# Decoding float64 weights with three VectorE instructions a piece, w1 ahead of the late part of w2

## The chip, the cores and the metric

The kernel runs on one core of one Trainium2 chip. A core has a matrix engine (TensorE, in the profile PE for matmuls and PEld for weight loads), VectorE (DVE), ScalarE (ACT), GpSimd (POOL) and SyncE (SP), whose queue issues nearly all DMAs here. Each engine runs its own instructions strictly in their order, and semaphores make one engine wait for another. The metric is device time of one execution in microseconds; the median of three runs of the kernel before is 1156.33 us (1154.52 to 1156.69).

## What is computed

Linear attention with random features on 8 batches, 8 heads, 576 tokens, 64 channels and 128 features; then a token mixing of rank 32 with a residual; then a two-layer MLP with relu and a residual. Inputs of the attention are float32; U, V, w_ch1 (w1, 512 x 2048) and w_ch2 (w2, 2048 x 512) come as float64.

```python
def phi(x):
    proj = np.einsum('bhsd,md->bhsm', x, omega)
    sq = np.sum(x * x, axis=-1, keepdims=True) / 2.0
    h = proj - sq
    h = h - np.max(h, axis=-1, keepdims=True)
    return np.exp(h) / np.sqrt(m)
q_p, k_p = (phi(q_s), phi(k_s))
kv = np.einsum('bhsm,bhsd->bhmd', k_p, v)
z = np.sum(k_p, axis=2)
num = np.einsum('bhsm,bhmd->bhsd', q_p, kv)
den = np.einsum('bhsm,bhm->bhs', q_p, z)[..., None] + 1e-06
...
xt = x.transpose(0, 2, 1)
h = xt @ U @ V
u = x + h.transpose(0, 2, 1)
ch = np.maximum(u @ w_ch1, 0.0) @ w_ch2
return (u + ch).astype(np.float32)
```

## The kernel before

**Attention.** A unit is a pair of batches and two heads; there are 16. A round takes the keys of one unit and the queries of another through nine tiles of 128 rows, one tile of each a step, so 16 rounds make 144 steps (and seven more that finish). In a step TensorE projects both tiles (L500 to L502, once for each of the two parts), VectorE takes the maximum (L508, tile nm), ScalarE the exponentials (L515, tile e), TensorE multiplies keys with values (L412) or transposes the queries' features (L438), VectorE or ScalarE copies those (L443), and TensorE combines them with kv (L458). Every three steps VectorE turns raw keys or queries (L373), ScalarE rounds them (L377) and GpSimd subtracts for the remainder (L381). The table `DELAY` says how many steps after its own each operation stands in the program.

**Mixing.** When a pair of batches is done, `mixing` takes nine tiles through U and V between the steps, with its subtraction on GpSimd (L261; on VectorE for the last pair) and an addition on VectorE (L276), and stores u to DRAM.

**MLP.** u comes back in 12 chunks of 384 tokens. An *item* is one chunk and one of 16 blocks of 128 hidden channels: 12 matmuls of the first layer (L682 to L684, tile p_p, two buffers), relu with rounding on ScalarE (L687, tile gh), its remainder on VectorE (L688, tile gl) and 9 matmuls of the second layer (L700), which stand behind the next item's first layer. There are 192 items. The first four take blocks 0 and 1 of chunks 0 and 1, and then these two chunks share each block, so that a row block f of w2 is first used at item 2f.

**Decoding.** `decoding` is a generator over 35 *pieces* of up to 512 float64 a row: U, two of V, 16 of w1, 16 of w2. A piece is loaded by SP into raw (two buffers, words interleaved); ScalarE takes the absolute value of the high words as a float into mag (L111, two buffers); VectorE clamps (L127), shifts and masks (L128), puts the sign back (L131), takes the power of two of the result (L134) and multiplies the low word by it (L135, tile de); GpSimd adds de to mag (L149); ScalarE rounds the sum to the high part and GpSimd subtracts for the low part (L162 and L163, for the weights). The generator yields after every VectorE instruction, so an `advance` is one of them. `left` counts the advances allowed before the late part of w2, which takes the place in SBUF of the mixing's tiles: 6 empty ones and 60 instructions, 12 pieces (U, V, w1's 0 to 5, w2's 0 and 1, w1's 6). In attention two of three steps advance once, which uses them up by step 99. The other 23 pieces come in the MLP, five instructions an item, w1 and w2 in turn.

**Order.** A scheduler sets each engine's order from the program's dependences and its own estimate of times; VectorE's decoding instructions and some copies are pinned to the program's order.

Of the kernel before, what the change touches and what calls it, by code (L numbers as in the profile page):

```python
# [9 lines left out]
F32 = mybir.dt.float32  # L10
F32R = mybir.dt.float32r
U32 = mybir.dt.uint32
AF = mybir.ActivationFunctionType
# [10 lines left out]
#: High words of the least and the greatest float64 with a normal float32's exponent.  # L24
# [4 lines left out]
def performer_mlp_kernel(ctx: ExitStack, tc, q, k, v, omega, U, V, w1, w2, out):  # L29
    """phi(q) (phi(k)^T v) / den, then x + V^T U^T x and a relu MLP with a residual.  # L30

    float32 products run natively or as float32r passes over operands split exactly into a
    rounded high part and the remainder. U, V, w1 and w2 come as the bits of float64 and are
    rounded to float32. The 2 x 576 rows of a pair of batches make nine tiles of 128, the fifth
    with the last 64 rows of one batch and the first 64 of the next.
    """
# [17 lines left out]
    # Both feature maps carry 1 / sqrt(M), which the quotient drops when the guard grows by M.  # L54
# [42 lines left out]
    def decoding(jobs, late=0):  # L97
        """jobs: (load, n, finish...); load(raw) fills [P, n, 2] with the words of n float64 in each
        row, and each finish(w) runs in turn on the float32 [P, n]. Yields after every VectorE
        instruction; loads run ahead."""  # L100
        raws, mags = {}, {}

        def fetch(i):
            if i < len(jobs):
                raws[i] = dec.tile([P, PIECE, 2], U32, name="raw", bufs=RB)[:, : jobs[i][1], :]
                jobs[i][0](raws[i])

        def magnitude(i):
            if i < len(jobs):
                mags[i] = dec.tile([P, PIECE], F32, name="mag", bufs=2)[:, : jobs[i][1]]  # L110
                nc.scalar.activation(out=mags[i], in_=f32(raws[i][:, :, 1]), func=AF.Abs)  # L111

        for i in range(RB):
            fetch(i)
        for _ in range(late):
            yield
        magnitude(0)
        rest = []
        for i, job in enumerate(jobs):
            n = job[1]  # L120
            raw, m = raws.pop(i), mags.pop(i)
            low, high = raw[:, :, 0], raw[:, :, 1]
            e = dec.tile([P, PIECE], F32, name="de", bufs=2)[:, :n]
            # The float32 of the high word's bits in m; the rest is the low word in units of 2^-52
            # of its power of two.
            slots = [
                lambda: nc.vector.tensor_scalar(m, m, _LEAST, _MOST, ALU.max, ALU.min),  # L127
                lambda: nc.vector.tensor_scalar(  # L128
                    words(m), words(m), 3, 0x3FFFFFFF, ALU.logical_shift_left, ALU.bitwise_and
                ),  # L130
                lambda: nc.vector.scalar_tensor_tensor(  # L131
                    words(m), high, 0xC0000000, words(m), ALU.bitwise_and, ALU.bitwise_or
                ),
                lambda: nc.vector.tensor_scalar(words(e), words(m), 0xFF800000, None, ALU.bitwise_and),  # L134
                lambda: nc.vector.scalar_tensor_tensor(e, low, 2.0**-52, e, ALU.mult, ALU.mult),  # L135
            ]
            for j, slot in enumerate(slots):
                tc.keep_in_program_order(slot())
                if rest:
                    rest.pop(0)()  # L140
                if j == 3:
                    magnitude(i + 1)
                if j == 4:
                    fetch(i + RB)
                yield
            while rest:
                rest.pop(0)()
            rest = [
                lambda e=e, m=m: nc.gpsimd.tensor_tensor(out=m, in0=m, in1=e, op=ALU.add),  # L149
            ]  # L150
            rest += [lambda fn=fn, m=m: fn(m) for fn in job[2:]]
        while rest:
            rest.pop(0)()
            yield
# [16 lines left out]
    # What the first steps of the MLP need, then the pieces of w1 and w2 in turn.  # L171
    N1, FIRST = DF // PIECE * NC, 6
# [15 lines left out]
    # U in columns [high, high, low, high], a slot for each tile of each batch: four of the first  # L188
    # batch, the shared tile's two with zeros in the other batch's rows, four of the second.
# [22 lines left out]
    # V in rows [high, high, high, low]; the shared tile has a slot for each batch.  # L212
# [27 lines left out]
    # Instructions of the decoder before the first that needs the late part of w2.  # L240
    left = [6 + 5 * (1 + 2 + FIRST + AHEAD + 1)]
# [8 lines left out]
    def mixing(pair, x, last):  # L250
        """A tile of x may be written as late as the one before it is used. The last pair's has the
        more of VectorE and of the banks."""
# [68 lines left out]
    def fetch(c, raws):  # L321
        """A chunk of u in 32 x 32 blocks that VectorE turns: row 32 a + i holds, for each block of 32
        tokens, 32 channels of block a of its token i."""
        for cc, raw in enumerate(raws):
            for a in range(4):
                k = cc * P + a * BLK
                nc.sync.dma_start(
                    out=raw[a * BLK : (a + 1) * BLK, :].rearrange("i (b j) -> i b j", j=BLK),
                    in_=u_dram[c][:, k : k + BLK].rearrange("(b i) j -> i b j", i=BLK),
                )  # L330

# [6 lines left out]
    # The third unit comes before the first buffer is free; the second of x is, till then.  # L338
# [7 lines left out]
    def blocks(src, raw, unit, j):  # L346
        """A batch of two heads in 32 x 32 blocks that VectorE turns: row 64 h + 32 a + i holds, for
        each block of 32 tokens, 32 channels of half a of its token i."""
        pair, hp = unit
        for h in range(2):  # L350
            for a in range(2):
                r = h * D + a * BLK
                nc.sync.dma_start(
                    out=raw[r : r + BLK, j * S : (j + 1) * S].rearrange("i (b c) -> i b c", c=BLK),
                    in_=src[2 * pair + j, 2 * hp + h, :, a * BLK : (a + 1) * BLK].rearrange("(b i) c -> i b c", i=BLK),
                )

    class Part:
        """Keys or queries of a unit, in the first or the second place of a round."""
# [9 lines left out]
        def turn(self):  # L369
            """The next group of tiles with channels on the partitions."""  # L370
# [12 lines left out]
    class Keys(Part):  # L383
        """phi(k)^T [v, 1] of two heads and two batches."""
# [37 lines left out]
    class Queries(Part):  # L422
        """The attention's output for two heads and two batches, into x."""

        def __init__(self, i, place):
# [4 lines left out]
            # The two of the last round share a bank for each tile, others one for two tiles.  # L430
# [32 lines left out]
        def finish(self, s, x):  # L463
# [7 lines left out]
            if s == 4:  # L471
                # Heads, then batches, of which a row has its own.
# [14 lines left out]
    class Step:  # L487
        """A step of a round: a tile of two heads from each of its parts."""
# [15 lines left out]
        # exp(h - max(h)): |x|^2 / 2 is one number for a row, so h - max(h) is proj - max(proj).  # L504
# [14 lines left out]
        def group(self, i):  # L519
            """Part i, when a group of tiles begins."""  # L520
# [11 lines left out]
    # Each round has two of the 32 parts: a unit's queries come two rounds after its keys but for  # L532
    # the first, and the first and the last round have two of a kind.
# [8 lines left out]
    # The tensor engine's clock goes up before its first work comes.  # L542
# [7 lines left out]
    for vt, vm in values:  # L550
        # Values with a column of ones for the denominator; the shared tile has a row's values
        # in its batch's columns and zeros in the other's.
# [19 lines left out]
    NR = len(units)  # L572
    # How many steps after its own a step's operation comes in the program.
# [9 lines left out]
    for s in range(NR * NT + 7):  # L583
# [17 lines left out]
        elif t == 7:  # L601
            # The MLP's first tokens, where the last pair but one was.
# [6 lines left out]
        if s % 3:  # L609
            advance(decoder)  # L610
# [52 lines left out]
    class Chunk:  # L663
# [28 lines left out]
        def layer2(self, f, gh, gl):  # L692
# [4 lines left out]
            for t, po in enumerate(self.po):  # L697
                ts = slice(t * P, (t + 1) * P)
                for i, (g, w) in enumerate(((gh, h), (gh, l), (gl, h))):
                    step = nc.tensor.matmul(po, g[:, ts], w, start=(f + i == 0), stop=(f == NF - 1 and i == 2))  # L700
                    if (self.c, f) == (NCH - 1, NF - 1):
                        # The last rows leave a tile at a time.
# [16 lines left out]
    # Two chunks share the first pass over the weights while these are decoded, then one a pass.  # L719
# [10 lines left out]
    def end(i):  # L730
        """The second layer of step i, behind the first of step i + 1."""
# [33 lines left out]
    for i in range(begun, len(items)):  # L765
        c, f = items[i]
        advance(decoder, 5, True)
# [37 lines left out]
```

## Time and profile before

| | |
|---|---|
| median of three runs | 1156.33 us |
| the profiled execution, from first to last instruction (span) | 1154.0 us |
| TensorE matmuls busy | 1123.9 us |
| mean granted TensorE clock | 0.991 |
| attention, first projection of step 0 to that of step 143 | 8.4 to 316.3 us |
| first matmul of MLP item 0 | 327.5 us |
| last piece decoded by VectorE | 456 us |

The profile's lines are read in this way. A window's row gives, for a stretch in microseconds, its length and then each engine's busy time with its number of instructions, the granted TensorE clock, the busy share of the DMA engines and GB/s. A group's row gives line, engine, operation, output and inputs with shapes and count, then busy time, mean duration in ns, and the idle time of the engine just before such instructions with what ended it. A row of waits gives who waited for whom, the total, how often and the longest. Overlapping matmuls make a busy TensorE look fuller than it is, so the number of matmuls in a stretch is read with it.

### The profile page before, as it was taken

To read this page: it belongs to the slowest core of one execution; us is meant where nothing else is said; L and a number is where in the kernel's file an instruction comes from. 1 tells how busy PE (TensorE), PEld (TensorE's weight loads), DVE (VectorE), ACT (ScalarE), POOL (GpSimd) and SP (SyncE) were. 2 spreads that over 40 slices of the span, in tenths; PEclk is the share of its full clock that TensorE was granted. 3 is DMA by queue.
4 is the path that set the end of the run, shared out by engine and by line. 5 is a ranking of instruction groups with operands and counts; after the bars stand their busy time and mean duration, and the time that the engine had idled before them with its cause. 6 is when DMAs were issued, how large, how long until landed. Compare 5 with 4: busy or idle time off the path is not lost.

```text
span 1154.0 us, 17600 instructions
## 1 busy us (share of the span) xinstructions
PE 1123.9 (97%) x6481; PEld 1020.8 (88%) x6481; DVE 538.6 (47%) x1088; ACT 405.3 (35%) x1115; POOL 280.7 (24%) x261
## 2 busy tenths in 40 slices
PE   8989999999999889999999999999999999999998
PEld 7989889899978677999999999999999999999997
DVE  3889999998997998411212121221212121111211
ACT  4978889788842333211111111111111111111111
POOL 3446657645244555201001010100101010010000
PEclk7999999999999999999999999999999999999999
DMA  7787686774356332420303030030303001010100
GB/s 131 141 152 138 139 180 132 155 157 89 93 146 154 106 106 74 105 61 5 78 1 83 1 74 10 7 75 1 83 1 82 1 1 55 1 55 1 46 1 28
DMA packets 288661, 84.95 MB, mean 74 GB/s; under 512 B 270368, under 2 KB 270368, under 8 KB 288576
## 3 DMA queue, kind: packets, MB, share of 16 engines
q1 hardware_dynamic: 288512, 83.77, 31.8%
q8 instruction: 51, 0.84, 0.3%
q14 instruction: 34, 0.28, 0.1%
q0 software_dynamic: 64, 0.07, 0.0%
HBM read 64.91 MB, written 18.87 MB: 73 GB/s over the span
## 4 chain that ended last, share of the span: by engine, by line
PE 71%; DVE 10%; DMA 2%; issue 1%; SPq 1%; ACT 1%; POOL 0%; DVEq 0%; ACTq 0%
PE p_p L683 10%; PE p_n L700 10%; PE p_p L684 10%; PE p_p L682 10%; PE p_q L700 10%; PE p_m L700 5%; PE p_kv L700 5%; PE p_n L458 2%; DVE mag L131 2%; PE p_kv L412 2%; DVE de L134 2%; DVE mag L128 2%; PE p_p L500 1%; PE p_q L438 1%; PE p_p L502 1%
## 5 line engine op out<-in xcount | busy, mean ns | idle before, releaser
L688 DVE SCALAR_TENSOR_TENSOR gl<-p_p,gh 128x384 fp32r<-128x384 f32 x192 | 106.8, 556 | 522.2 <-ACT gh L687 521.9
L687 ACT ACTIVATE gh<-p_p 128x384 fp32r<-128x384 f32 x192 | 94.0, 490 | 570.1 <-PE p_p L684 569.1
L682 PE MATMUL p_p<-uh,w1h 128*128 128x384 f32 x768 | 258.5, 337 | 1.7 <-DVE gl L688 1.3
L683 PE MATMUL p_p<-uh,w1l 128*128 128x384 f32 x768 | 258.8, 337 | 0.0
L684 PE MATMUL p_p<-ul,w1h 128*128 128x384 f32 x768 | 258.1, 337 | 0.0
L515 ACT ACTIVATE e<-p_p,nm 128x128 f32<-128x128 f32 x576 | 166.4, 385 | 39.8 <-DVE nm L508 30.7
L676 POOL TENSOR_TENSOR ul<-uT,uh 128x384 fp32r<-128x384 f32 x48 | 48.4, 1039 | 537.2 <-ACT uh L675 537.2
L682 PEld LDWEIGHTS p_p<-uh,w1h 128*128 128x128 f32 x768 | 144.2, 188 | 11.2 <-DVE gl L688 2.0
L683 PEld LDWEIGHTS p_p<-uh,w1l 128*128 128x128 f32 x768 | 144.1, 188 | 9.1
L684 PEld LDWEIGHTS p_p<-ul,w1h 128*128 128x128 f32 x768 | 144.0, 188 | 0.3
L381 POOL TENSOR_TENSOR xl<-xT,xh 128x384 fp32r<-128x384 f32 x96 | 102.4, 1083 | 125.5 <-ACT xh L377 92.8
L508 DVE TENSOR_REDUCE nm<-p_p 128x4 f32<-128x512 f32 x144 | 98.1, 682 | 23.7 <-PE p_p L502 14.5
L500 PE MATMUL p_p<-omh,xh 128*128 128x256 f32 x288 | 94.2, 327 | 1.2 <-ACT e L515 0.9
L501 PE MATMUL p_p<-oml,xh 128*128 128x256 f32 x288 | 82.4, 286 | 0.0
L502 PE MATMUL p_p<-omh,xl 128*128 128x256 f32 x288 | 82.3, 286 | 0.0
L458 PE MATMUL p_n<-kv,eT 128*128 128x65 f32 x512 | 74.7, 273 | 7.1 <-DVE eT L443 3.3
L700 PE MATMUL p_n<-w2h,gl 128*128 128x512 f32 x192 | 76.6, 399 | 3.4 <-DVE gl L688 3.3
L458 PEld LDWEIGHTS p_n<-kv,eT 128*128 128x128 f32 x512 | 68.5, 193 | 12.0 <-DVE eT L443 6.4
L700 PE MATMUL p_n<-w2h,gh 128*128 128x512 f32 x192 | 75.8, 395 | 1.9 <-ACT gh L687 1.1
L700 PE MATMUL p_n<-w2l,gh 128*128 128x512 f32 x192 | 75.8, 395 | 0.3 <-POOL w2l L163 0.2
L700 PE MATMUL p_q<-w2l,gh 128*128 128x512 f32 x192 | 75.1, 392 | 0.0
L700 PE MATMUL p_q<-w2h,gl 128*128 128x512 f32 x192 | 75.0, 395 | 0.0
(106 smaller groups left out, 1863.4 us busy)
## 6 DMA issues: line engine op xcount, KB each, us to landing
raw<-in_moe_w_ch_dram SPq DMA_DIRECT2D x32, 512.0 KB, 3.8
u_dram<-ut SPq DMA_DIRECT2D x36, 256.0 KB, 2.3
u<-u_dram SPq DMA_DIRECT2D x36, 256.0 KB, 3.8
out_dram<-u SPq DMA_DIRECT2D x36, 256.0 KB, 2.5
kt<-in_k_dram SPq DMA_DIRECT2D x120, 72.0 KB, 2.6
qt<-in_q_dram SPq DMA_DIRECT2D x120, 72.0 KB, 2.7
uraw<-u_dram SPq DMA_DIRECT2D x176, 48.0 KB, 2.3
vt<-in_v_dram SPq DMA_DIRECT2D x60, 128.0 KB, 2.7
```

The lines of the kernel that those rows point to most:

```text
L381: nc.gpsimd.tensor_tensor(out=self.xl[-1], in0=self.turned, in1=f32(self.xh[-1]), op=ALU.subtract)
L458: nc.tensor.matmul(pn[:, h, :], eT[:, h, :], kv[:, h, s // 5, :], start=True, stop=True)
L500: nc.tensor.matmul(o, part.xh[g][:, ts], oh, start=True, stop=False)
L502: nc.tensor.matmul(o, part.xl[g][:, ts], oh, start=False, stop=True)
L508: nc.vector.tensor_reduce(out=self.nm[:, :n], in_=self.pp[:, :n], axis=AX.X, op=ALU.max, negate=True)
L515: nc.scalar.activation(out=self.e[:, j, :], in_=self.pp[:, j, :], func=AF.Exp, bias=self.nm[:, j : j + 1])
L682: nc.tensor.matmul(ph, w1h[:, cc, fs], self.uh[cc], start=(cc == 0), stop=False)
L683: nc.tensor.matmul(ph, w1l[:, cc, fs], self.uh[cc], start=False, stop=False)
L684: nc.tensor.matmul(ph, w1h[:, cc, fs], self.ul[cc], start=False, stop=(cc == NC - 1))
L687: nc.scalar.activation(out=self.gh, in_=ph, func=AF.Relu)
L688: nc.vector.scalar_tensor_tensor(out=self.gl, in0=ph, scalar=0.0, in1=f32(self.gh), op0=ALU.max, op1=ALU.subtract)
L700: step = nc.tensor.matmul(po, g[:, ts], w, start=(f + i == 0), stop=(f == NF - 1 and i == 2))
```

## The change

A piece now has three VectorE instructions. ScalarE makes a second operation beside the absolute value: it reads the low words as unsigned integers, multiplies them by 2^-29 and writes int32 to a new tile low (two buffers). GpSimd adds low to the bits of mag as integers. The two VectorE instructions that made de (L134, L135) and the tile de are gone. ScalarE's pair for the next piece is issued after the second instruction of a piece (before: after the fourth), and the load after next behind the third (before: the fifth).

All 16 pieces of w1 are decoded ahead of w2 (`FIRST` is 16, before 6), so that after w2's first two pieces only w2 follows. `left` becomes 72: 6 empty advances and 66 instructions, 22 pieces (U, V, w1, w2's 0 to 2). In attention every second step advances once, up to step 143. In the MLP 13 pieces are left, three instructions an item.

```diff
-    N1, FIRST = DF // PIECE * NC, 6
+    N1, FIRST = DF // PIECE * NC, DF // PIECE * NC
...
-        def magnitude(i):
+        def units(i):
             if i < len(jobs):
-                mags[i] = dec.tile([P, PIECE], F32, name="mag", bufs=2)[:, : jobs[i][1]]
+                n = jobs[i][1]
+                mags[i] = dec.tile([P, PIECE], F32, name="mag", bufs=2)[:, :n]
+                lows[i] = dec.tile([P, PIECE], I32, name="low", bufs=2)[:, :n]
                 nc.scalar.activation(out=mags[i], in_=f32(raws[i][:, :, 1]), func=AF.Abs)
+                nc.scalar.activation(out=lows[i], in_=raws[i][:, :, 0], func=AF.Copy, scale=2.0**-29)
...
-                lambda: nc.vector.tensor_scalar(words(e), words(m), 0xFF800000, None, ALU.bitwise_and),
-                lambda: nc.vector.scalar_tensor_tensor(e, low, 2.0**-52, e, ALU.mult, ALU.mult),
             ]
...
-                if j == 3:
-                    magnitude(i + 1)
-                if j == 4:
+                if j == 1:
+                    units(i + 1)
+                if j == 2:
                     fetch(i + RB)
...
             rest = [
-                lambda e=e, m=m: nc.gpsimd.tensor_tensor(out=m, in0=m, in1=e, op=ALU.add),
+                lambda m=m, low=low: nc.gpsimd.tensor_tensor(
+                    out=m.bitcast(I32), in0=m.bitcast(I32), in1=low, op=ALU.add
+                ),
             ]
...
-    left = [6 + 5 * (1 + 2 + FIRST + AHEAD + 1)]
+    left = [6 + 3 * (1 + 2 + FIRST + AHEAD + 1)]
...
-        if s % 3:
+        if s % 2:
             advance(decoder)
...
-        advance(decoder, 5, True)
+        advance(decoder, 3, True)
```

The scheduler makes new orders of this. In the rows below, line numbers of the changed kernel are its own, 4 higher for what is unchanged (L127 is L131 there, L131 is L135, L688 is L692).

VectorE in the second half of attention, before; nm is the maximum, eT the copied features, rec and x the quotient, xT the turned raw tile:

```order
L508 TENSOR_REDUCE nm<-p_p 128x4
L373 STREAM_TRANSPOSE xT<-kt 128x384
L373 STREAM_TRANSPOSE xT<-qt 128x384
L508 TENSOR_REDUCE nm<-p_p 128x4
L468 TENSOR_SCALAR rec<-p_n 128x4
L443 COPY eT<-p_q 128x256
L469 RECIPROCAL rec<-rec 128x4
L483 TENSOR_TENSOR x<-p_n,rec 128x2x128
```

The same engine and part of the program, changed:

```order
L377 STREAM_TRANSPOSE xT<-kt 128x384
L132 TENSOR_SCALAR mag<-mag 128x512
L377 STREAM_TRANSPOSE xT<-qt 128x384
L472 TENSOR_SCALAR rec<-p_n 128x4
L512 TENSOR_REDUCE nm<-p_p 128x4
L473 RECIPROCAL rec<-rec 128x4
L447 COPY eT<-p_q 128x256
L487 TENSOR_TENSOR x<-p_n,rec 128x2x128
L512 TENSOR_REDUCE nm<-p_p 128x4
L135 SCALAR_TENSOR_TENSOR mag<-raw,mag 128x512
```

A decoding instruction stands in every second step there, where before none did.

GpSimd in the MLP's decoding, before; L149 is the addition to mag, L163 the subtraction for the low part of a weight:

```order
L149 TENSOR_TENSOR mag<-mag,de 128x512
L163 TENSOR_TENSOR w1l<-mag,w1h 128x512
L149 TENSOR_TENSOR mag<-mag,de 128x512
L163 TENSOR_TENSOR w2l_5669<-mag,w2h_5668 128x512
L149 TENSOR_TENSOR mag<-mag,de 128x512
```

And changed:

```order
L151 TENSOR_TENSOR mag<-mag,low 128x512 x2
L167 TENSOR_TENSOR w2l_5781<-mag,w2h_5780 128x512
L167 TENSOR_TENSOR w2l_5783<-mag,w2h_5782 128x512
L151 TENSOR_TENSOR mag<-mag,low 128x512 x2
L167 TENSOR_TENSOR w2l_5785<-mag,w2h_5784 128x512
L167 TENSOR_TENSOR w2l_5787<-mag,w2h_5786 128x512
```

Two pieces now go through GpSimd together: both additions, then both subtractions.

ScalarE at the end of the MLP's decoding, changed; gh is an item's relu, w2h a weight's high part, mag and low the two operations on a loaded piece:

```order
L166 CAST w2h_5792<-mag 128x512
L118 ACTIVATE low<-raw 128x512
L691 ACTIVATE gh<-p_p 128x384
L166 CAST w2h_5794<-mag 128x512
L117 ACTIVATE mag<-raw 128x512
L118 ACTIVATE low<-raw 128x512
L117 ACTIVATE mag<-raw 128x512
L691 ACTIVATE gh<-p_p 128x384
L166 CAST w2h_5796<-mag 128x512
L166 CAST w2h_5798<-mag 128x512
L691 ACTIVATE gh<-p_p 128x384 x15
```

The last late copy (w2h_5798) has 15 gh of items ahead of it; in the kernel before, the last one has 26.

More of the change, by code (lines that the diff above doesn't have):

```diff
@@ L12 @@
 U32 = mybir.dt.uint32
+I32 = mybir.dt.int32
 AF = mybir.ActivationFunctionType
@@ L97, in decoding @@
     def decoding(jobs, late=0):
-        raws, mags = {}, {}
+        raws, mags, lows = {}, {}, {}
         def fetch(i):
@@ L116, in decoding @@
             yield
-        magnitude(0)
+        units(0)
         rest = []
@@ L120, in decoding @@
             n = job[1]
-            raw, m = raws.pop(i), mags.pop(i)
-            low, high = raw[:, :, 0], raw[:, :, 1]
-            e = dec.tile([P, PIECE], F32, name="de", bufs=2)[:, :n]
+            raw, m, low = raws.pop(i), mags.pop(i), lows.pop(i)
+            high = raw[:, :, 1]
             slots = [
```

## The prediction

> **What bounds the kernel now.** First the page's totals: TensorE is nearly always busy.
>
> ```profile
> span 1154.0 us, 17600 instructions
> PE 1123.9 (97%) x6481; PEld 1020.8 (88%) x6481; DVE 538.6 (47%) x1088; ACT 405.3 (35%) x1115; POOL 280.7 (24%) x261
> ```
>
> A busy share does not say whether matmuls come as fast as they can, so next the busy time of each engine in five stretches: attention steps 36 to 98 (with decoding), steps 99 to 143 (without it), the last mixing with MLP items 0 to 6, items 7 to 25 (with decoding), and a long piece of plain MLP. Then the same stretches for two lines alone: L500 runs twice a step, L682 four times an item.
>
> ```profile
> core 0: us, PE busy (x) PEld busy (x) DVE busy (x) ACT busy (x) POOL busy (x), PEclk, DMA share, GB/s
> 88.10:227.40 139.30, 134.22 (x1066) 124.47 (x1066) 134.10 (x308) 116.53 (x367) 91.25 (x76) 1.00 0.71 146
> 227.40:316.30 88.90, 88.28 (x747) 85.47 (x747) 79.09 (x201) 76.04 (x249) 38.93 (x37) 1.00 0.54 118
> 316.30:359.20 42.90, 41.45 (x215) 34.88 (x214) 37.25 (x80) 17.84 (x39) 16.96 (x15) 1.00 0.63 156
> 359.20:455.40 96.20, 85.06 (x401) 70.30 (x399) 91.08 (x116) 32.47 (x58) 55.89 (x40) 1.00 0.36 107
> 513.80:972.80 459.00, 459.00 (x2311) 416.43 (x2310) 90.00 (x159) 68.41 (x138) 27.66 (x28) 1.00 0.14 35
> ```
>
> ```profile
> 88.10:227.40 139.30, 40.38 (x126) 23.96 (x127) 1.00 0.71 146
> 227.40:316.30 88.90, 27.72 (x89) 16.83 (x89) 1.00 0.54 118
> ...
> 359.20:455.40 96.20, 25.77 (x77) 14.27 (x76) 1.00 0.36 107
> 513.80:972.80 459.00, 147.88 (x440) 82.62 (x440) 1.00 0.14 35
> ```
>
> Plain MLP does 110 items in 459.0 us, **4.173 us an item**, with VectorE a fifth busy: TensorE is the bound there. The decoding stretch does 19 items in 96.2 us, 5.06 each, with VectorE 95% busy (91.08): VectorE is the bound, and 96.2 - 19 x 4.173 = **16.9 us** are lost. That is what the change can win in the MLP. In attention, steps 36 to 98 have VectorE at 134.10 of 139.30 (96%) and take 2.21 us each; steps 99 to 143, without decoding, take 1.98 with VectorE at 89% and TensorE at 99%. So VectorE work in the first costs time, and the second has 9.8 us of idle VectorE in all.
>
> What a decoding instruction costs, by stretch (attention 60 to 250 us, then items 7 to 25), from the groups by line; columns: busy us, mean ns, idle before:
>
> ```profile
> L131 DVE SCALAR_TENSOR_TENSOR mag<-raw,mag 128x512 uint32<-128x512 uint32 (+1 forms) x10 | 11.1, 1110 | 0.0
> L135 DVE SCALAR_TENSOR_TENSOR de<-raw,de 128x512 f32<-128x512 uint32 (+1 forms) x10 | 8.4, 844 | 0.0
> ...
> L128 DVE TENSOR_SCALAR mag<-mag 128x512 uint32<-128x512 uint32 x9 | 7.6, 843 | 0.0
> L127 DVE TENSOR_SCALAR mag<-mag 128x512 f32<-128x512 f32 x9 | 7.6, 840 | 0.0
> ...
> L134 DVE TENSOR_SCALAR de<-mag 128x512 uint32<-128x512 uint32 (+1 forms) x10 | 6.7, 667 | 0.0
> ```
>
> ```profile
> L149 POOL TENSOR_TENSOR mag<-mag,de 128x512 f32<-128x512 f32 x20 | 27.7, 1385 | 29.5 <-DVE de L135 29.5
> ...
> L134 DVE TENSOR_SCALAR de<-mag 128x512 uint32<-128x512 uint32 x20 | 20.1, 1003 | 0.5
> L128 DVE TENSOR_SCALAR mag<-mag 128x512 uint32<-128x512 uint32 x19 | 19.7, 1037 | 0.5
> L131 DVE SCALAR_TENSOR_TENSOR mag<-raw,mag 128x512 uint32<-128x512 uint32 x19 | 19.5, 1024 | 0.6
> L163 POOL TENSOR_TENSOR w2l<-mag,w2h 128x512 fp32r<-128x512 f32 x12 | 17.9, 1488 | 8.8 <-ACT w2h L162 8.8
> ...
> L135 DVE SCALAR_TENSOR_TENSOR de<-raw,de 128x512 f32<-128x512 uint32 x20 | 13.8, 691 | 0.6
> ...
> L127 DVE TENSOR_SCALAR mag<-mag 128x512 f32<-128x512 f32 x19 | 12.2, 641 | 2.8 <-ACT mag L111 2.8
> L688 DVE SCALAR_TENSOR_TENSOR gl<-p_p,gh 128x384 fp32r<-128x384 f32 x19 | 10.5, 550 | 0.1
> ```
>
> The means hide two values, as a moment of the timeline shows (VectorE, then GpSimd):
>
> ```profile
> 382.73 0.41 DVE L127 TENSOR_SCALAR mag<-mag 128x512 f32<-128x512 f32 x1
> 383.18 1.41 DVE L128 TENSOR_SCALAR mag<-mag 128x512 uint32<-128x512 uint32 x1
> 384.62 0.69 DVE L131 SCALAR_TENSOR_TENSOR mag<-raw,mag 128x512 uint32<-128x512 uint32 x1
> 385.37 0.56 DVE L688 SCALAR_TENSOR_TENSOR gl<-p_p,gh 128x384 fp32r<-128x384 f32 x1
> 385.85 0.91 DVE L134 TENSOR_SCALAR de<-mag 128x512 uint32<-128x512 uint32 x1
> ```
>
> ```profile
> 382.89 1.41 POOL L149 TENSOR_TENSOR mag<-mag,de 128x512 f32<-128x512 f32 x1 [1.43 <-DVE de L135]
> ```
>
> A tensor_scalar takes 0.41 us free; L128, begun while a GpSimd operation ran (to 384.30), ended 0.29 us behind it. Free, the five cost 0.41 + 0.41 + 0.69 + 0.41 + 0.69 = 2.61 us; the means in attention sum to 4.30 and in the MLP to 4.40, so about 1.7 us of a piece is waiting behind GpSimd.
>
> **The change, part by part.** All terms are made against the profiled execution (span 1154.0, 2.3 us under the 1156.33 median; I carry the difference over).
>
> *MLP, items 7 to 25.* Three decoding instructions and the remainder L688 cost VectorE 0.64 + 1.04 + 1.02 + 0.55 = 3.25 us an item, under 4.17. What is next late is the piece's own chain: GpSimd's rows stand add, add, subtract, subtract, and two buffers of mag tie a pair of pieces to the pair before. From one pair's first subtraction to the next's: second subtraction 1.49, a blocked tensor_scalar's rest 0.29, the free one 0.41, L131 0.69, add 1.39, the second piece's blocked tensor_scalar 0.29, L688 0.55, L131 0.69, add 1.39, subtraction 1.49: 8.68 us a pair, 4.34 an item, 0.17 over TensorE's pace. VectorE and ScalarE are in order, so L688 and L687 queue behind these waits, and TensorE waits for them. ScalarE's new order (shown above) has 15 L687 ahead of the last late copy, so decoding ends with item 14, so 8 items carry it here: between 8 x 0.17 = 1.4 and 8 x 0.89 = 7.1 us (today's pace). I take 0.4 each, nearer the chain: 3.2 us. **Term: 3.2 - 16.9 = -13.7** (bounds -16.9 and -9.8).
>
> *The stretch 316.3 to 359.2.* TensorE is 97% busy there; fewer VectorE instructions can give what it idles, 1.5 us, and perhaps as much again if its matmuls then come closer. **Term: -1** (0 to -3).
>
> *Attention, steps 36 to 98.* An advance in every second step, not two in three: 42 instructions become 31.5. Neighbours overlap by 0.08 us (L688 above ends at 385.93, the next starts at 385.85), so of the mean 0.86 of all five 0.78 counts, and of the kept three's 0.93, 0.85: 31.5 x 0.85 - 42 x 0.78 = -6.0 us of VectorE. ScalarE gets more, by these rows:
>
> ```profile
> L111 ACT ACTIVATE mag<-raw 128x512 f32<-128x512 f32 x10 | 7.0, 704 | 5.7 <-DMA raw<-in_moe_w_ch_dram 5.2 <-POOL w1l L163 0.3 <-POOL w2l L163 0.2
> ...
> L162 ACT CAST w1h<-mag 128x512 fp32r<-128x512 f32 x6 | 3.9, 650 | 0.0
> ```
>
> ```profile
> L111 ACT ACTIVATE mag<-raw x14: 479/682/804, 35.2 to 340.5; 128x512 f32<-128x512 f32 x11, 128x288 f32<-128x288 f32 x2, 128x320 f32<-128x320 f32 x1
> ```
>
> The new low-word operation reads the same stride as L111; I take that one's mean, 0.70, with the 0.65 of L162 and the longest L111, 0.80 (the second fence: min/median/max), as bounds: -1.1 to +2.2 us on the 22 pieces. [...] Pieces go from 8.4 at 1.35 to 10.5 at 2.06, ScalarE from 116.5 to 126.8. TensorE at the pace of the next stretch (747 matmuls in 88.9) needs 1066 x 0.119 = 126.9, VectorE 128.1. Three engines at 127 to 128 us, each waiting for the others, will not reach 133.3. **Term: -3** (-6 to +1).
>
> *Attention, steps 99 to 143.* Decoding is new here: 22.5 instructions, 19.1 us, on VectorE's 79.1 is 98.2 against 88.9. At 96% busy that is 102.3; with all blocking gone, 22.5 x 0.43 = 9.7 us, it would be 88.8. GpSimd gets 7.5 pieces at some 2.6 us on its 38.9: 59% busy, near the 66% of the stretch before, so blocking stays. **Term: +9.5** (0 to +13.4).
>
> *Before 88 us* the pieces are small: nothing, -3 to +4 (ScalarE waited 5.2 us for raw in the row above, and that may come elsewhere). The integer add on GpSimd is in no row; the 128x512 rows L149 and L163 give 1.39 and 1.49, and the shortest two-input one, on 32x288, 0.81; I take 1.39, the float add's:
>
> ```profile
> L229 POOL TENSOR_TENSOR sv<-mag,sv 32x288 fp32r<-32x288 f32 x1 | 0.8, 806 | 1.0 <-ACT sv L226 1.0
> ```
>
> At 0.81 a pair would be 1.16 shorter (3.76 an item, TensorE's pace), at 1.49 0.2 longer (0.8 us in all); both lie in the bounds of the first term.
>
> *Loads.* Ten more weight loads stand in SP's queue among attention's loads of keys and queries, where DMAs are busy 71% and 54%:
>
> ```profile
> raw<-in_moe_w_ch_dram SPq DMA_DIRECT2D x32, 512.0 KB, 3.8
> ```
>
> A piece's ScalarE operations now come some 4 steps (8 us) after its load, not 6: still twice 3.8, so I take nothing. Where a load is late, ScalarE waits at the head of its queue with the exponentials behind it; that is in the +4 above.
>
> Taking w1 first costs nothing: its pieces are done before item 0, and w2's row f is copied by about item f + 1 and used at item 2f.
>
> **Sum:** -13.7 - 1 - 3 + 9.5 = **-8.2 us**: span 1145.8, time **1148**.
>
> **Rivals.**
> 1. *ScalarE becomes attention's bound (slower).* It is in order, and each piece now puts 0.70 us more ahead of the exponentials (L515) that TensorE waits for. If all 22 land on the path: 15.4 us, -8.2 + 15.4 = +7.2, **1163**. It decides when more than 8.2 of the 15.4 does. For it: 126.8 of about 136 us busy. Against: 16% idle now, and this row of the waits in 88 to 227 us, ScalarE waiting for VectorE:
>
> ```profile
> ACT e L515 <- DVE nm L508: 12.8, 19, 1.9
> ```
>
> 2. *The waiting stays with the pieces.* If each GpSimd operation blocks one VectorE instruction, whichever comes, three kept instructions wait as long as five did: 1.51 + 1.69 = 3.20 us a piece in attention, not 2.79. Over 18 pieces 7.4 us: **1155.5**, no change. [...]
> 3. *The piece chain keeps today's 5.06 us an item* for all 13 late pieces: 11.6 us lost, 5.3 saved; with attention +6.5 **1157**. An integer add longer than a float one would do it.
> 4. *Attention evens out and the MLP recovers whole:* -6 + 9.3 - 15.5 - 3 = -15, **1141**.
>
> **How the numbers follow.** Forecast 0.42 (own range 1143 to 1153), rival 1 0.21, rival 2 0.12, rival 3 0.10, rival 4 0.15. A measurement can tell some 0.2%, 2.3 us. Faster: forecast, rival 4, a sixth of rival 2: 0.59; slower: rival 1; within: 0.20. The range 1139 to 1164 reaches past rivals 4 and 1.
>
> **What would show it.** Items 7 to 14 at 4.2 to 4.7 us and 4.173 from there; steps 36 to 98 at 2.15 to 2.2 us and steps 99 to 143 at 2.1 to 2.25 with VectorE over 94% busy. Wrong: mean L127, L128 and L131 summing to 3.2 in attention (rival 2); ScalarE over 95% busy with VectorE waiting for exponentials (rival 1); GpSimd's integer add above 1.6 us (rival 3).

## The result, and the profile after

| | before | after |
|---|---|---|
| median (4 runs each) | 1155.94 us | 1171.4 us (1169.62 to 1174.38) |
| ratio to before | | **1.0134** (95% interval 1.0115 to 1.0153) |
| span of the profiled execution | 1154.0 us | 1167.8 us |

The change makes the kernel 1.3% slower. The page of the changed kernel, totals of the engines:

```profile
span 1167.8 us, 17560 instructions
PE 1129.7 (97%) x6481; PEld 1027.0 (88%) x6481; DVE 480.0 (41%) x1018; ACT 421.8 (36%) x1150; POOL 270.2 (23%) x261
```

VectorE has lost 58.6 us of work (538.6 before) and the time has grown all the same. The stretches are cut at the same steps and items as before: steps 36 to 98, steps 99 to 143, up to item 6, items 7 to 25, and 110 items of plain MLP.

```profile
core 0: us, PE busy (x) PEld busy (x) DVE busy (x) ACT busy (x) POOL busy (x), PEclk, DMA share, GB/s
90.90:237.40 146.50, 135.01 (x1062) 124.92 (x1062) 129.50 (x300) 124.17 (x383) 93.67 (x82) 0.99 0.70 147
237.40:340.50 103.10, 94.90 (x751) 88.44 (x749) 92.74 (x220) 86.42 (x268) 58.12 (x52) 0.98 0.58 133
340.50:384.90 44.40, 41.71 (x217) 34.90 (x217) 32.92 (x71) 18.69 (x42) 15.87 (x14) 1.00 0.66 152
384.90:469.30 84.40, 81.43 (x401) 71.38 (x400) 32.07 (x50) 27.80 (x51) 28.61 (x23) 1.00 0.22 63
527.60:986.60 459.00, 459.00 (x2312) 416.43 (x2311) 89.95 (x159) 68.41 (x138) 27.66 (x28) 1.00 0.14 35
```

Against before: +2.8 us ahead of step 36, 146.5 - 139.3 = +7.2, 103.1 - 88.9 = +14.2, 44.4 - 42.9 = +1.5, 84.4 - 96.2 = -11.8, plain MLP the same. So the MLP wins most of what was hoped for (11.8 of 13.7 us) and attention loses 24.2 us. There no engine is full: in the first stretch VectorE is busy 88%, ScalarE 85%, TensorE 92%. An engine that is not full and yet late is waiting, so the next view is that of the waits in attention (90.9 to 340.5 us), ScalarE's and then TensorE's; columns: total us, how often, the longest.

```profile
ACT low L118 <- DMA raw<-in_moe_w_ch_dram: 17.4, 16, 3.0
...
ACT e L519 <- DVE nm L512: 4.6, 12, 0.5
```

```profile
PE p_q L442 <- ACT e L519: 14.3, 16, 2.6
```

ScalarE now waits 16 times for a piece's load, 17.4 us in all, at its new operation on the low words; TensorE waits 16 times for the exponentials, 14.3 us. In the kernel before, ScalarE waited for VectorE in these steps; it waited once for a load, and TensorE three times, shortly, for these exponentials (88.1 to 316.3 us):

```profile
ACT e L515 <- DVE nm L508: 19.3, 31, 1.9
...
ACT mag L111 <- DMA raw<-in_moe_w_ch_dram: 1.6, 1, 1.6
```

```profile
PE p_q L438 <- ACT e L515: 0.7, 3, 0.3
```

A moment of the timeline of the changed kernel shows the two together: the load's issue on SP, then ScalarE, then TensorE.

```profile
152.15 0.44 SPq L162 DMA_DIRECT2D raw<-in_moe_w_ch_dram  x1
```

```profile
153.69 0.95 ACT L381 CAST xh<-xT 128x384 fp32r<-128x384 f32 x2
157.60 0.66 ACT L118 ACTIVATE low<-raw 128x512 int32<-128x512 uint32 x1 [2.96 <-DMA raw<-in_moe_w_ch_dram]
158.16 1.13 ACT L519 ACTIVATE e<-p_p,nm 128x128 f32<-128x128 f32 x4
...
162.72 0.73 ACT L117 ACTIVATE mag<-raw 128x512 f32<-128x512 f32 x1
```

```profile
158.57 0.33 PE L442 MATMUL p_q<-ident,e 128*128 128x128 f32 x1 [2.63 <-ACT e L519]
```

The load is issued at 152.15 and lands 5.4 us later. ScalarE has nothing else to do from 154.64 on, because the head of its queue is the operation on the low words of that piece; four exponentials stand behind it, and TensorE, which needs them, idles for 2.63 us. The absolute value of the same piece starts only at 162.72: it would not have waited. The order of ScalarE's instructions in the changed kernel has low behind mag for the first five pieces; from the sixth on (86.5 us) low stands ahead at every piece of attention, for example:

```
L118 ACTIVATE low<-raw 128x512
L264 CAST mh<-x 128x512
L519 ACTIVATE e<-p_p,nm 128x128 x4
...
L447 COPY eT<-p_q 128x256
L117 ACTIVATE mag<-raw 128x512
```

The program writes the pair as mag, low; the scheduler took low apart and moved it ahead.

### The profile page after: what moved, and what is told of

It is laid out like the page before. It is cut to its first block, busy times and chain, and to the rows that moved or that the text cites. A ratio compares the mean times of both kernels' runs of the same rounds, so it can differ in the third digit from the quotient of the medians.

```text
span 1167.8 us, 17560 instructions
## 1 busy us (share of the span) xinstructions
PE 1129.7 (97%) x6481; PEld 1027.0 (88%) x6481; DVE 480.0 (41%) x1018; ACT 421.8 (36%) x1150; POOL 270.2 (23%) x261
## 4 chain that ended last, share of the span: by engine, by line
PE 74%; DMA 8%; DVE 6%; ACT 4%; issue 4%; SPq 3%; POOL 1%; DVEq 0%; ACTq 0%; POOLq 0%
PE p_n L704 11%; PE p_p L687 11%; PE p_p L688 11%; PE p_p L686 11%; PE p_q L704 11%; PE p_m L704 5%; DMA raw<-in_moe_w_ch_dram 5%; PE p_kv L704 5%; ACT e L519 2%; PE p_n L462 2%; SPq L357 2%; PE p_p L504 2%; PE p_q L442 2%; PE p_kv L416 1%; DVE nm L512 1%
## 5 line engine op out<-in xcount | busy, mean ns | idle before, releaser
L692 DVE SCALAR_TENSOR_TENSOR gl<-p_p,gh 128x384 fp32r<-128x384 f32 x192 | 106.8, 556 | 568.4 <-ACT gh L691 568.0
L688 PE MATMUL p_p<-ul,w1h 128*128 128x384 f32 x768 | 258.1, 337 | 0.0
L688 PEld LDWEIGHTS p_p<-ul,w1h 128*128 128x128 f32 x768 | 144.0, 188 | 0.1
L385 POOL TENSOR_TENSOR xl<-xT,xh 128x384 fp32r<-128x384 f32 x96 | 96.2, 1016 | 88.2 <-ACT xh L381 61.2
L504 PE MATMUL p_p<-omh,xh 128*128 128x256 f32 x288 | 96.2, 334 | 2.1 <-ACT e L519 1.8
L442 PE MATMUL p_q<-ident,e 128*128 128x128 f32 x288 | 63.3, 288 | 16.1 <-ACT e L519 15.3
L704 PE MATMUL p_q<-w2h,gh 128*128 128x512 f32 x192 | 75.3, 393 | 0.0
```

The costliest lines, as they stand in the source:

```text
L385: nc.gpsimd.tensor_tensor(out=self.xl[-1], in0=self.turned, in1=f32(self.xh[-1]), op=ALU.subtract)
L442: nc.tensor.transpose(pq[:, j, :], e[:, j, :], ident)
L504: nc.tensor.matmul(o, part.xh[g][:, ts], oh, start=True, stop=False)
L688: nc.tensor.matmul(ph, w1h[:, cc, fs], self.ul[cc], start=False, stop=(cc == NC - 1))
L692: nc.vector.scalar_tensor_tensor(out=self.gl, in0=ph, scalar=0.0, in1=f32(self.gh), op0=ALU.max, op1=ALU.subtract)
```

## The experiments

Three theories stood at the start. **1:** the place of the low operation in ScalarE's queue, so the wait for the load. **2:** the work that it adds to ScalarE (rival 1 of the prediction). **3:** VectorE's decoding in steps 99 to 143. All ratios are against runs of the kernel before on the same chip; "step 143" is its first projection in the profiled execution (316.3 us before, 340.5 in the changed kernel).

| run | time, us | ratio (95%) | step 143, us |
|---|---|---|---|
| new order, low behind mag (every second step) | 1153.8 | 0.9973 (0.9961 to 0.9985) | 325.6 |
| no low operation | 1144.84 | 0.9900 (0.9883 to 0.9916) | 319.7 |
| low on 8 columns | 1166.88 | 1.0093 (1.0064 to 1.0122) | 338.8 |
| before, early reader | 1169.58 | 1.0101 (1.0067 to 1.0136) | 323.1 |
| before, reader behind mag | 1160.4 | 1.0028 (1.0019 to 1.0038) | 315.6 |
| the same, wider tile | 1155.17 | 0.9987 (0.9977 to 0.9997) | 315.3 |
| new order, low behind mag, two of three steps | 1156.01 | 0.9988 (0.9975 to 1.0001) | 329.6 |
| order of before, low behind mag, two of three steps | **1143.64** | **0.9882** (0.9861 to 0.9903) | 315.2 |
| order of before, low behind mag, every second step | **1143.22** | **0.9875** (0.9849 to 0.9900) | 317.3 |
| that one, ScalarE's pair issued later | 1143.86 | 0.9888 (0.9869 to 0.9907) | 313.2 |
| that one, 8 pieces of w1 first | 1145.04 | 0.9892 (0.9878 to 0.9907) | 315.9 |
| that one, low free again | 1150.09 | 0.9945 (0.9926 to 0.9965) | 321.2 |

**The low operation kept behind the absolute value.**

```diff
-                nc.scalar.activation(out=lows[i], in_=raws[i][:, :, 0], func=AF.Copy, scale=2.0**-29)
+                tc.keep_in_program_order(
+                    nc.scalar.activation(out=lows[i], in_=raws[i][:, :, 0], func=AF.Copy, scale=2.0**-29)
+                )
```

> The changed kernel with one edit: ScalarE's low-word operation is kept behind the absolute value of the same piece; in the changed kernel the scheduler has it 6 to 9 steps of the queue ahead of it. Same work, same DMAs. Theory 1 (in the changed kernel ScalarE stands in its queue at the low operation until the piece's load has landed, 17.4 us in 16 waits between 90.9 and 340.5 us, with the exponentials behind it): these waits go to under 2 us, attention's step 143 comes 15 to 20 us earlier (320 to 326 us instead of 340.5), time 1151 to 1157. Theory 2 (the 0.67 us a piece that the operation costs ScalarE is what lengthens attention): 1168 to 1173. Theory 3 (VectorE's decoding in steps 99 to 143, and its mix with the rest, is what lengthens it): 1168 to 1173.

Its stretches, cut at the same steps and items as above, then a row of ScalarE's waits and one of TensorE's in 89.3 to 325.6 us:

```profile
89.30:227.10 137.80, 131.70 (x1063) 123.19 (x1063) 130.08 (x300) 124.32 (x385) 94.52 (x82) 1.00 0.75 155
227.10:325.60 98.50, 92.77 (x747) 86.32 (x746) 92.07 (x222) 85.75 (x268) 58.63 (x51) 1.00 0.61 142
325.60:368.80 43.20, 41.66 (x217) 35.08 (x216) 32.69 (x71) 18.79 (x43) 15.50 (x14) 1.00 0.67 156
368.80:451.30 82.50, 80.40 (x400) 71.29 (x399) 31.49 (x49) 27.41 (x50) 28.91 (x23) 1.00 0.21 64
```

```profile
ACT e L521 <- DVE nm L514: 13.3, 17, 2.9
```

```profile
PE p_q L444 <- ACT e L521: 2.2, 6, 0.6
```

ScalarE does the same work (124.32 and 85.75 us busy, 124.17 and 86.42 before this edit), but no wait for a load is left in these stretches; ScalarE waits for VectorE again, as in the kernel before, and TensorE's 14.3 us for exponentials are 2.2. Step 143 comes 14.9 us earlier, at the lower edge of the 15 to 20 that theory 1 gave, and the span is 1167.8 - 1150.2 = 17.6 us shorter. Theories 2 and 3 had said that this edit would change nothing. In items 7 to 25, too, low had waited for loads in the changed kernel, 11.3 us in 9 waits; there the edit gives only 84.4 - 82.5 = 1.9 us, so these waits of ScalarE cost the time 1.9 us, not their own length.

**No low operation**, and **the low operation on 8 of 512 columns**.

```diff
+    zero = dec.tile([P, PIECE], I32, name="low")
+    nc.gpsimd.memset(zero, 0)
...
-                lows[i] = dec.tile([P, PIECE], I32, name="low", bufs=2)[:, :n]
+                lows[i] = zero[:, :n]
...
-                nc.scalar.activation(out=lows[i], in_=raws[i][:, :, 0], func=AF.Copy, scale=2.0**-29)
```

> The changed kernel without the low-word operation: a tile that is zeroed once takes its place in GpSimd's addition, so the low words of the weights are left out. ScalarE loses both the wait and 35 operations of 0.67 us. Theories 1 and 2: step 143 at 313 to 324 us, time 1142 to 1155; the difference to the run with the operation kept behind the absolute value prices ScalarE's work alone (theory 1: at most 5 us, theory 2: 15 us or more). Theory 3: attention keeps most of its 24 us, time 1160 to 1170.

```diff
+    fixed = [dec.tile([P, PIECE], I32, name=f"low{i}") for i in range(2)]
+    for t in fixed:
+        nc.gpsimd.memset(t, 0)
...
-                lows[i] = dec.tile([P, PIECE], I32, name="low", bufs=2)[:, :n]
+                lows[i] = fixed[i % 2][:, :n]
...
-                nc.scalar.activation(out=lows[i], in_=raws[i][:, :, 0], func=AF.Copy, scale=2.0**-29)
+                nc.scalar.activation(out=lows[i][:, :8], in_=raws[i][:, :8, 0], func=AF.Copy, scale=2.0**-29)
```

> The changed kernel with the low-word operation on 8 columns of a piece instead of 512, into two fixed tiles zeroed once, so most of the low words are left out. ScalarE's work for it is nearly gone, but it still reads the load and still stands ahead of the absolute value. Theory 1: the waits for the load stay (12 us or more in attention), time 1162 to 1171. Theory 2: attention is back by 15 us or more, 1148 to 1157. Theory 3: 1166 to 1172.

The low operation on 8 columns, its group between 60 and 338.8 us and its row of the waits from 87.6 on:

```profile
L122 ACT ACTIVATE low<-raw 128x8 int32<-128x8 uint32 x21 | 4.4, 209 | 23.2 <-DMA raw<-in_moe_w_ch_dram 22.4 <-POOL ml L269 0.7
```

```profile
ACT low L122 <- DMA raw<-in_moe_w_ch_dram: 22.4, 17, 4.0
```

With a third of the work (0.21 us instead of 0.67) the waits are longer, 22.4 us, and the ratio is 1.0093, where the changed kernel has 1.0134 and low behind mag 0.9973: it is not mainly the work. Without the operation the time is 0.7% below the run that keeps it behind the absolute value (8.4 us by the ratios, 5.5 by the two spans): the work is not free, but it is under half of what the early place costs. That is more than the 5 us that theory 1 allowed and far from theory 2's 15.

**The wait alone, put into the kernel before.** An idle reader of the load, free to move; then the same reader kept behind the absolute value.

```diff
                 nc.scalar.activation(out=mags[i], in_=f32(raws[i][:, :, 1]), func=AF.Abs)
+                peek = dec.tile([P, 8], F32, name="peek", bufs=2)
+                nc.scalar.activation(out=peek, in_=f32(raws[i][:, :8, 1]), func=AF.Abs)
```

> The kernel before with one more, idle, ScalarE operation a piece: the absolute value of 8 of the piece's columns into a tile that nothing reads, written behind the piece's absolute value and free for the scheduler to move, as the low operation was; it stands ahead of the absolute value for the pieces from about step 30 on. Everything else is the kernel before. Theory 1 (an early reader of the load blocks ScalarE until it has landed): some 8 pieces in attention wait 0.5 to 1.5 us each with the exponentials behind them, and attention's step 143 comes 4 to 12 us later than 316.3; time 1160 to 1168. Rival (the early reader costs only where ScalarE is also loaded with the new operation): 1155 to 1158, no change.

```diff
-                nc.scalar.activation(out=peek, in_=f32(raws[i][:, :8, 1]), func=AF.Abs)
+                tc.keep_in_program_order(nc.scalar.activation(out=peek, in_=f32(raws[i][:, :8, 1]), func=AF.Abs))
```

> Control for the idle early reader in the kernel before: the same operation on 8 columns, kept behind the piece's absolute value. Theory 1 (what cost there was the place in ScalarE's queue, so the wait for the load): the cost goes, step 143 within 3 us of 316.3, time 1154 to 1160. Rival (the operation itself, or the longer hold of the load's buffer, costs): 1163 to 1172 as with the early place.

The early reader: steps 36 to 98, and the waits there of ScalarE and TensorE:

```profile
88.10:234.70 146.60, 135.95 (x1067) 127.03 (x1066) 135.72 (x313) 118.22 (x381) 90.45 (x77) 0.98 0.68 142
```

```profile
ACT peek L113 <- DMA raw<-in_moe_w_ch_dram: 13.9, 7, 3.6
```

```profile
PE p_q L440 <- ACT e L517: 7.4, 5, 2.1
```

The reader kept behind, the same steps and TensorE's row:

```profile
87.70:226.60 138.90, 132.63 (x1068) 124.35 (x1066) 134.15 (x310) 117.93 (x376) 91.34 (x77) 1.00 0.71 146
```

```profile
PE p_q L440 <- ACT e L517: 0.4, 2, 0.2
```

So an operation of 0.2 us (207 ns, the mean of 11) that nothing needs lengthens these steps by 7.7 us when it stands early, and by nothing when it stands late (138.9, 139.3 without it). Theory 1 holds without anything else of the change. Both times lie above what was expected (1160 to 1168 and 1154 to 1160), as both runs took some 4.5 us more than the kernel before behind item 26; the last section comes back to it.

**The order of before, with three instructions**, and its spread and place varied. The first run's edit, beside the low operation kept behind:

```diff
-    N1, FIRST = DF // PIECE * NC, DF // PIECE * NC
+    N1, FIRST = DF // PIECE * NC, 6
...
-        if s % 2:
+        if s % 3:
```

> Three VectorE instructions a piece and the low operation kept behind the absolute value, but the order of the pieces and the share of attention's steps of the kernel before (w1 and w2 in turn, 12 pieces in attention, an advance in two of three steps, so 42 advances, used up by step 62). Theory (steps 99 to 143 lengthen by the decoding that was moved there, 1.3 us a piece, while a late piece costs the MLP 0.25 us): steps 36 to 98 in 128 to 134 us, steps 99 to 143 in 88 to 91, items 7 to 25 in 82 to 87; time 1131 to 1144. Rival (the new order is what makes the MLP's decoding short): items 7 to 25 stay at 90 us or more, time 1142 to 1152.

> As the run with the order of before, with an advance in every second step (42 advances, used up by step 83). Thinner decoding leaves VectorE more room a step, but as many instructions: 1131 to 1144, within 3 us of the other.

The changed kernel's order with `s % 3`:

> The changed kernel with the low operation kept behind the absolute value and an advance in two of three steps, so that the 22 pieces of attention are done by step 108. Theory: the 9.6 us of steps 99 to 143 shrink to 2 to 4, steps 36 to 98 get 0 to 5 us longer than the 137.8 of the thin spread; the MLP as there: 1147 to 1154. If VectorE's total decides and not its place, it stays at 1152 to 1156.

Steps 36 to 98 and 99 to 143 with the order of before (12 pieces in attention):

```profile
93.50:227.50 134.00, 130.52 (x1069) 123.07 (x1068) 121.16 (x288) 116.77 (x369) 80.55 (x71) 1.00 0.72 146
227.50:315.20 87.70, 87.51 (x745) 84.97 (x745) 77.07 (x198) 75.93 (x250) 38.93 (x37) 1.00 0.51 111
```

And with the new order (22 pieces), the same spread:

```profile
93.30:238.90 145.60, 137.17 (x1063) 124.22 (x1062) 139.87 (x309) 129.71 (x394) 106.57 (x88) 1.00 0.80 162
238.90:329.60 90.70, 89.35 (x749) 86.10 (x748) 81.74 (x207) 78.92 (x255) 43.47 (x40) 1.00 0.57 122
```

These two differ in `FIRST` alone, which sets both the order and how many pieces attention takes; the two were not varied apart. Ten pieces more in attention bring step 143 from 315.2 to 329.6 us, 1.44 us a piece; from item 0 to item 26 the MLP takes 117.1 us with them late and 115.5 with them early, 0.16 a piece. The 1.44 is a mean of this pair of runs: with an advance in every second step the same ten bring step 143 from 317.3 to 325.6, 0.83 a piece, and two pieces more (the second variant below) did not delay it. Decoding this far ahead is the wrong direction: the MLP has VectorE to spare (in the second of these runs it is busy 30.64 of 83.2 us in items 7 to 25), attention has not (139.87 of 145.60 in steps 36 to 98). The thinner spread doesn't help: with 22 pieces it only moves the loss (137.8 and 98.5 against 145.6 and 90.7), and with 12 the two times cannot be told apart. The expectation for two of three steps was missed: 1156.0, where its rival said 1152 to 1156. That for the order of before held, near its upper end, as steps 0 to 35 took 5 us more than before; why they did is open.

**Three variants** of the order of before with every second step: ScalarE's pair issued behind the third instruction, with the absolute value kept in the program's order too; 8 pieces of w1 first; the low operation free again.

```diff
-                nc.scalar.activation(out=mags[i], in_=f32(raws[i][:, :, 1]), func=AF.Abs)
+                tc.keep_in_program_order(nc.scalar.activation(out=mags[i], in_=f32(raws[i][:, :, 1]), func=AF.Abs))
...
-                if j == 1:
+                if j == 2:
                     units(i + 1)
-                if j == 2:
                     fetch(i + RB)
```

> The order of before with three instructions and an advance in every second step, and ScalarE's pair for the next piece issued after the third instruction instead of the second, both kept in the program's order, so 6 steps behind the load instead of 4. Theory: the two waits left for the load (4.6 us of ScalarE between 49 and 94 us in the run with the earlier pair) go, steps 0 to 35 take 80 to 82 us instead of 84.6, time 1138 to 1142. Rival: in the MLP the pair then comes too late for VectorE and items 7 to 25 lengthen by 3 us or more: 1143 to 1150.

> The order of before with three instructions, an advance in every second step and 8 instead of 6 pieces of w1 ahead of w2's (14 pieces in attention, 21 late). Attention pays 1.4 us for each of the two (+2.9); items 5 to 8, which took 3.0 us more than four at 4.173 in the run with 6, can give back up to that: 1141 to 1147.

> The order of before with three instructions and an advance in every second step, but the low operation free for the scheduler, which puts it 4 to 7 places of ScalarE's queue ahead of the absolute value. Theory 1: ScalarE waits for the load at each of the 9 full pieces of attention, 1.1 us each, and with what follows from it attention is 7 to 14 us longer: 1149 to 1158. Rival (it matters only with the new order of pieces): 1142 to 1146.

The first won 6.3 us ahead of step 36 in its profile (78.2 from step 0, not 84.6) and gave back 2.6 in steps 36 to 98 and 1.1 up to item 6. Its median is no better and misses the 1138 to 1142 expected, ScalarE's waits for a load were still 3.9 us, and items 7 to 25 did not lengthen as its rival had it (84.9 us, not 84.4): inconclusive. The second gave 1145.04, but neither of its reasons held: attention was not longer (step 143 at 315.9), and items 0 to 6 took 33.3 us instead of 31.6. The third repeats the main finding with the old order: 8 waits for a load, 8.1 us in all, and a time 0.7% longer. Step 143 comes only 3.9 us later, though, where 7 to 14 had been expected.

## Why the prediction was wrong

The step that failed is under *Loads*: "A piece's ScalarE operations now come some 4 steps (8 us) after its load, not 6: still twice 3.8, so I take nothing." That is true of the absolute value: with low kept behind it, both start 7.7 us or more behind the load's issue in attention from the third piece of w1 on, without a wait. It is not true of the low operation where the scheduler had put it: between 95 and 335 us it came to the head of ScalarE's queue 2.3 to 4.2 us behind the issue, one to two steps, and the load let it start only 3.7 to 5.5 us behind it. The rows of the order in the section on the change already show a low operation parted from its absolute value, with an item's relu between them; the prediction read them only for where decoding ends. It then put late loads into a bound of +4 us ahead of 88 us, where the wait costs 17.6 us over the whole kernel.

With that one operation back in its place (the first experiment) the rest can be read term by term, in us:

| term of the sum | forecast (bounds) | low behind mag | changed kernel |
|---|---|---|---|
| before step 36 | 0 (-3 to +4) | +1.2 | +2.8 |
| steps 36 to 98 | -3 (-6 to +1) | -1.5 | +7.2 |
| steps 99 to 143 | +9.5 (0 to +13.4) | +9.6 | +14.2 |
| up to item 6 | -1 (-3 to 0) | +0.3 | +1.5 |
| items 7 to 25 | -13.7 (-16.9 to -9.8) | -13.7 | -11.8 |

So the other terms held, but for the fourth, 0.3 us above its bounds. Together they are -4.1 us, not -8.2, and the forecast of 1148 would have been 4 to 6 us too low even so: 1153.8. Two of the close hits are partly luck. The +9.6 comes from 92.07 us of VectorE work in a stretch that it filled to 93%; the sum had 98.2 us of work there. And the 0.4 us an item lost in items 7 to 14 was a choice between 0.17 and 0.89; it came out at 0.40, but no run tests the chain of a pair of pieces that gave the 0.17. A slip that changes little: from step 99's first projection to step 143's there are 44 steps, 2.02 us each before, not the 1.98 of the prediction.

The rivals, by the groups of the changed kernel between 60 and 340.5 us:

```profile
L132 DVE TENSOR_SCALAR mag<-mag 128x512 uint32<-128x512 uint32 x19 | 19.0, 1002 | 0.0
L135 DVE SCALAR_TENSOR_TENSOR mag<-raw,mag 128x512 uint32<-128x512 uint32 x19 | 16.2, 853 | 0.1
L131 DVE TENSOR_SCALAR mag<-mag 128x512 f32<-128x512 f32 x19 | 15.0, 788 | 2.3 <-ACT mag L117 2.2
```

```profile
L118 ACT ACTIVATE low<-raw 128x512 int32<-128x512 uint32 x21 | 14.1, 671 | 18.9 <-DMA raw<-in_moe_w_ch_dram 17.6 <-POOL xl L385 0.7 <-POOL ml L265 0.6
```

```profile
L151 POOL TENSOR_TENSOR mag<-mag,low 128x512 int32<-128x512 int32 x19 | 24.3, 1278 | 15.1 <-DVE mag L135 8.6 <-DVE rec L472 6.5
```

- **Rival 1** (slower, ScalarE) came nearest: exponentials were late behind a piece's operation. But its price was the operation's 0.70 us, and its sign "ScalarE over 95% busy" did not show (85% and 84%). The operation takes 0.67; what was late was the data it reads. Its work alone costs 5.5 to 8.4 us (the run without it), not 15.4.
- **Rival 2** fell: the three kept instructions sum to 1.00 + 0.85 + 0.79 = 2.64 us, less than the 2.79 of the sum and far from 3.20. Of 1.69 us of waiting a piece 1.13 is left, so waiting behind GpSimd goes with the instructions, though not quite in proportion (three fifths would be 1.01). In the changed kernel between 60 and 340.5 us L132 takes 0.38 or 0.39 us in 4 of its 19 cases and 0.83 to 1.32 us in the 15 that began while a GpSimd operation ran; each of these ended 0.28 or 0.29 us behind that operation, as the one at 383.18 did before. How much waiting another mix of instructions keeps, no run shows.
- **Rival 3** fell: the integer add takes 1.28 us. Items 7 to 14 take 38.1 / 8 = 4.77 us in the changed kernel, just above the 4.2 to 4.7 that was named, and 4.57 with low behind mag; from item 15 on 4.20 and 4.18.
- **Rival 4** fell with its first half: attention did not even out.

## What to carry to other kernels

An operation that reads a DMA's result must be looked for in its engine's own order, not in the program: here it stood 2.3 to 4.2 us behind the load's issue, and what was behind it waited with it for the landing, 17.4 us in 16 waits; on 8 columns, at 0.21 us, it waited 22.4 us in 17. When an operation on loaded data is added to a busy in-order engine, tie it behind the last instruction that already needs that load: here this brought step 143 from 340.5 to 325.6 us. And before work is moved ahead, price a piece where it goes and where it comes from: here 0.83 to 1.44 us, by the spread, against 0.16 to 0.18.

## What else the runs showed of the hardware

**A stall of 2.49 us, with half the clock behind it.** The changed kernel around a wait of 2.49 us of TensorE for exponentials that ends at 258.04, in windows of 2 us:

```profile
256.00:258.00 2.00, 0.00 (x0) 0.00 (x0) 0.46 (x3) 1.34 (x4) 0.20 (x1) 1.00 1.12 211
258.00:260.00 2.00, 1.96 (x15) 1.84 (x16) 1.20 (x5) 2.00 (x8) 0.79 (x1) 0.93 1.05 145
260.00:262.00 2.00, 2.00 (x12) 2.00 (x12) 1.97 (x4) 1.62 (x7) 1.27 (x1) 0.50 0.69 152
262.00:264.00 2.00, 2.00 (x15) 2.00 (x15) 1.48 (x5) 1.64 (x5) 1.43 (x2) 0.72 0.15 31
264.00:266.00 2.00, 2.00 (x20) 2.00 (x19) 1.92 (x6) 1.99 (x8) 0.67 (x2) 1.00 0.10 24
```

TensorE is back at 258, but some 2 us later its granted clock falls to 0.50 and 12 matmuls go in 2 us, not 20. The three windows miss 2 x (0.07 + 0.50 + 0.28) = 1.7 us of full clock; in windows of 0.5 us the clock is 0.72 in the one from 259.5, 0.50 in all six from 260 to 263 and 0.86 in the next, so some 3.4 us were at half. The wait of 2.63 us in the timeline above has no such spell behind it (the clock is 1.00 from 158 to 168); the other spell (174 to 178 us, with 0.50 in all six windows of 0.5 us from 174.5 to 177.5) has a wait of 1.75 us ahead of it. Why one wait is followed by a spell and a longer one is not, no run shows. Between 90.9 and 340.5 us the changed kernel has these two spells, which lose 1.7 us of full clock each; with low behind mag the granted clock is 1.00 in both stretches. That the stalls bring the spells is read from their place alone; no run tests it.

**A tile of 32 bytes a row slowed all of the MLP.** Plain MLP with the reader kept behind and its tile of 8 columns, then the same with a tile of 128 columns of which 8 are used:

```diff
-                peek = dec.tile([P, 8], F32, name="peek", bufs=2)
+                peek = dec.tile([P, 128], F32, name="peek", bufs=2)[:, :8]
```

> The control with the idle reader behind the absolute value, in which its tile has 128 columns (8 used) instead of 8. In both runs with the tile of 8 columns an item of the plain MLP takes 4.20 us and not 4.173 (4.5 us from item 26 to the end), though nothing of the MLP differs but where its tiles lie, since a tile of 32 bytes a row shifts those behind it. If the place of the tiles in SBUF is the reason, tiles of 512 bytes give 4.173 us an item again and 698.6 us from item 26 to the end, and the time is 1154 to 1158. If an additional tile or operation as such is the reason, 703 us and 1159 to 1162 as before.

```profile
513.80:972.80 459.00, 459.00 (x2297) 416.20 (x2296) 89.56 (x158) 68.00 (x137) 27.57 (x28) 1.00 0.14 35
...
L684 PE MATMUL p_p<-uh,w1h 128*128 128x384 f32 x438 | 148.6, 339 | 0.0
```

```profile
513.80:972.80 459.00, 459.00 (x2311) 416.42 (x2310) 90.10 (x159) 68.42 (x138) 27.61 (x28) 1.00 0.14 35
...
L684 PE MATMUL p_p<-uh,w1h 128*128 128x384 f32 x441 | 148.2, 336 | 0.0
```

With the small tile 14 matmuls fewer fit into 459 us, those of the first layer take 339 ns and not 336, and from item 26 to the end it is 703.1 us against 698.6. With the wide one the 698.6 are back, and the reader kept behind costs nothing (0.9987). So here the width of an idle tile decided, not its operation; that it acts through where the tiles behind it lie was the author's guess and is not shown, and which tile it is was not tried.
